# Four engines instead of one in written order: a scheduling change in the attention phase of a transformer block

## The chip, the core and the metric

The kernel runs on one core of one Trainium2 chip. The metric is device microseconds of one execution, smaller being better. Five engines work side by side, each through its own queue in order: TensorE (PE; its weight loads are listed as PEld), VectorE (DVE), ScalarE (ACT), GpSimd (POOL), and SyncE (SP), which here only issues DMA transfers. ScalarE's queue can issue transfers too. An instruction starts when the one ahead of it in its queue has started its turn and the semaphores that it waits for have been raised.

## The reference

Tokens S = 2048, width D = 576, one batch. Six vectors come from a condition vector `c`; a sliding-window attention block A and an MLP-mixer block B follow, each on a layer-normalised and modulated copy of x.

```python
mod = (silu(c) @ w_mod).reshape(1, 6, 1, D)
sa, ca, ga, sb, cb, gb = ...                      # its six rows
h = layernorm(x) * (1 + ca) + sa
x = x + ga * A(h)                                 # attention
h = layernorm(x) * (1 + cb) + sb
x = x + gb * B(h)                                 # mixer and MLP, F = 4608

# A: 32 heads of 18 columns, each token sees the 256 tokens up to itself
q, k, v = split(h @ wqkv)
p = softmax(where(0 <= i - j < 256, q @ k.T * 18 ** -0.5, -1e9))
A = (p @ v) @ wo
```

## The kernel before

All matrix products are kept close to float32 accuracy by writing each operand as a rounded high half and a low half (raw minus high half) and adding three products, so a contraction over 576 rows takes 14 matmuls (`products`). Making the two halves of an operand is called a split: ScalarE rounds (`split`, line 93), another engine subtracts (line 94).

Phase A (`phase_a`) is the attention. Tokens are treated in NB = 4 groups of 512. For each group the rows are normalised (`x_norm`: statistics on VectorE, lines 101 to 103, two small steps on GpSimd, 104 and 105, the scaling on ScalarE, 111), transposed on TensorE (`x_tr`, line 304), scaled and shifted by ScalarE (309), and split into `hT` by GpSimd (312) and VectorE (313). From `hT` nine q, k chunks of 128 columns (`qk_item`, line 321, 14 matmuls of 512 columns each) and eight v halves (`v_item`, 14 of 288 columns) are made. A q, k chunk leaves its PSUM bank through ScalarE and VectorE (lines 93 and 94, tile `qe`), goes to DRAM by transfers that ScalarE's queue issues (lines 348 to 354), and comes back rearranged by head (`pack`, lines 386 and 388, on SP's queue).

The attention itself is done in 32 units `u`, four heads and one group each. `scores` makes 16 score blocks of 128 x 384 (line 402); after each VectorE adds a mask and takes the row maximum (403). The maxima are negated, transposed and stored as two more rows of Q (`fin1`, `fin2`). `attend` makes the scores once more, transposed and with the maximum subtracted (436) and masked (445), ScalarE takes the exponential (449), TensorE multiplies with V (460), ScalarE copies the result out (465), and it is transposed and divided by its sum.

Beside this, `modvec` makes four of the modulation vectors on GpSimd (lines 492 and 494) from five loads each, and `s4` takes finished rows through the output projection: transposes and splits (71 to 79), 2 x 14 matmuls (627), addition of x (628), two normalisations with the modulation between them on GpSimd (638 and 639), stores. `load_w1` and `load_w2` bring and split the weights of the next phase. Phase B (`phase_bc`, `phase_b`) is the mixer, phase C (`phase_c`) the MLP.

The order of the work is written by hand: every step is put into a list `ev` with a time, whose unit is one attention unit u, and `play` calls them in the order of these times. `win` gives the stretches in which a group's projections are spread, `o_p`, `o_x`, `o_a` the offsets of loads, exponentials and products with V. For TensorE this order is binding:

```python
with self.tc.manual_schedule(engines={mybir.EngineType.PE}):
    play(ev)
```

The other queues are ordered by the framework's scheduler, which takes the written order as a priority and places what it estimates to be ready. In PSUM, `self.pb` gives the number of banks of each kind: `sc` 2 for score blocks, `st` 2 for the transposed scores, `av` 1, `mm` 2 for projections, `tr` 1 for transposes.

## Time and profile before

| what | value |
|---|---|
| median of three runs | 1886.11 us (1885.86 to 1888.06) |
| the profiled execution's own time | 1890.93 us |
| its span, first to last instruction | 1888.8 us |
| mean granted TensorE clock | 0.971 of full speed |
| busy: PE, DVE, ACT, POOL | 1774.5, 939.0, 635.6, 396.1 us |
| first copy of line 465 (end of the first unit) | 110.55 us |
| last copy of line 465 (end of the 32nd unit) | 783.22 us |

Busy times are sums over the whole span. A matmul of 128 x 512 is shown with about 0.4 us, but matmuls are pipelined, so a TensorE that is shown busy is not TensorE at its peak. In rows that list an instruction, the part in brackets is the idle time of its engine just ahead of it and what ended that; `x` with a number is how many instructions a row stands for.

### The profile page before, as it was taken

How to read it: one execution, taken by the hardware profiler on the slowest of the kernel's cores; microseconds unless marked ns; L12 is line 12 of the kernel's file. 1: busy time of each engine (PE TensorE's matmuls, PEld its weight loads, DVE VectorE, ACT ScalarE, POOL GpSimd, SP SyncE). 2: the span in 40 equal slices, each digit the busy share in tenths (PEclk: the TensorE clock that was granted, in tenths of full speed). 3: DMA queues.
4: the chain of work that ended last, by engine and by line, in shares of the span. 5: the costliest groups of instructions: out<-in, count | busy, mean ns of one | idle time of the engine just before them, and what ended most of it. 6: DMA issues, size and time to landing. Idle time of an engine off the chain costs nothing.

```text
span 1888.8 us, 29893 instructions
## 1 busy us (share of the span) xinstructions
PE 1774.5 (94%) x11504; PEld 1505.6 (80%) x11504; DVE 939.0 (50%) x2543; ACT 635.6 (34%) x1169; POOL 396.1 (21%) x430
## 2 busy tenths in 40 slices
PE   5889999999998888799989999999999999999999
PEld 3756766777776666588889999999999999999998
DVE  5445566555666666376754334343433434343333
ACT  3244454444554444443322222222222222222211
POOL 5030121111001222211232333332322222221100
PEclk7979999999999989899999999999999999999999
DMA  5533444424445443443421111110111000000002
GB/s 166 178 122 124 123 122 148 128 86 123 142 136 156 146 138 110 132 139 108 123 83 34 45 47 45 52 52 26 50 49 34 27 28 27 27 27 8 1 1 101
DMA packets 128117, 161.17 MB, mean 85 GB/s; under 512 B 35044, under 2 KB 69860, under 8 KB 127976
## 3 DMA queue, kind: packets, MB, share of 16 engines
q1 hardware_dynamic: 112616, 136.32, 24.7%
q10 hardware_dynamic: 15360, 22.95, 3.6%
q8 instruction: 91, 1.49, 0.3%
q14 instruction: 50, 0.41, 0.1%
HBM read 107.81 MB, written 50.73 MB: 84 GB/s over the span
## 4 chain that ended last, share of the span: by engine, by line
PE 80%; DVE 6%; DMA 5%; POOL 5%; issue 2%; ACT 2%; ACTq 0%; SPq 0%; POOLq 0%; DVEq 0%
PE p L911 24%; PE p L936 24%; PE qk L321 5%; PE sc L402 4%; PE X L436 4%; PE av L460 3%; PE pg L786 3%; PE po L627 2%; PE v L321 2%; PE X L445 2%; PE w L837 2%; DVE sc L403 1%; DMA wm<-in_w_mod_dram 1%; POOL s4rows L638 1%; POOL s4rows L639 1%
## 5 line engine op out<-in xcount | busy, mean ns | idle before, releaser
L911 PE MATMUL p<-LNT,W 128*128 128x512 f32 x2016 | 483.6, 391 | 0.0
L936 PEld LDWEIGHTS p<-W,Gc 128*128 128x128 f32 x3456 | 472.6, 188 | 11.1
L936 PE MATMUL p<-W,Gc 128*128 128x288 f32 x3456 | 480.4, 295 | 0.0
L911 PEld LDWEIGHTS p<-LNT,W 128*128 128x128 f32 x2016 | 372.0, 188 | 69.5
L403 DVE CUSTOM_DVE_ANT_0 sc<-sc,mask 128x384 f32<-128x384 f32 (+2 forms) x512 | 272.4, 541 | 188.7 <-PE sc L402 185.5
L915 ACT ACTIVATE gfc<-p 128x512 f32<-128x512 f32 x144 | 86.0, 597 | 663.4 <-PE p L911 663.4
L940 DVE TENSOR_TENSOR accA<-p,accA 128x288 f32<-128x288 f32 x340 | 151.5, 453 | 316.2 <-PE p L936 314.2
L449 ACT ACTIVATE P<-X 128x512 f32<-128x512 f32 (+2 forms) x384 | 216.2, 571 | 273.9 <-PE X L445 220.8
L402 PE MATMUL sc<-K,Q 108*128 108x384 f32 (+2 forms) x512 | 203.2, 399 | 33.7 <-DVE m L403 25.1
L940 DVE TENSOR_TENSOR accB<-p,accB 128x288 f32<-128x288 f32 x204 | 92.6, 455 | 198.1 <-PE p L936 196.1
L436 PE MATMUL X<-Q,K 110*128 110x128 f32 (+2 forms) x704 | 168.6, 315 | 11.0 <-ACT P L449 8.8
L321 PE MATMUL qk<-hT,Wc 128*128 128x512 f32 x504 | 163.4, 425 | 2.3 <-DVE hT L313 2.3
L436 PEld LDWEIGHTS X<-Q,K 110*128 110x128 f32 x704 | 128.2, 197 | 46.3 <-ACT P L449 17.9
L402 PEld LDWEIGHTS sc<-K,Q 108*128 108x128 f32 x512 | 101.0, 198 | 63.5 <-DVE m L403 39.8
L94 POOL TENSOR_TENSOR W<-r,W 128x576 fp32r<-128x576 f32 x34 | 49.1, 1443 | 466.8 <-ACT W L93 466.8
L445 PE MATMUL X<-maskb,identb 128*128 128x256 bf16 (+1 forms) x640 | 123.6, 259 | 0.0
L918 DVE TENSOR_TENSOR Gc<-gfc,Gc 128x512 fp32r<-128x512 f32 x144 | 118.2, 821 | 8.4 <-ACT Gc L917 4.7
L460 PE MATMUL av<-P,V 128*32 128x384 f32 (+2 forms) x1408 | 103.2, 406 | 0.0
L321 PEld LDWEIGHTS qk<-hT,Wc 128*128 128x128 f32 x504 | 88.8, 198 | 16.4 <-issue 4.8
L917 ACT CAST Gc<-gfc 128x512 fp32r<-128x512 f32 x144 | 89.3, 620 | 3.6
L321 PE MATMUL v<-Wv,hT 128*128 128x288 f32 x448 | 81.6, 305 | 0.5 <-ACT V L373 0.5
L627 PE MATMUL po<-Wo,oT 128*128 128x288 f32 x448 | 72.0, 312 | 2.1 <-DVE oT L79 1.5
(966 smaller groups left out, 1696.8 us busy)
## 6 DMA issues: line engine op xcount, KB each, us to landing
K<-k0d SPq DMA_DIRECT2D x96, 108.0 KB
r<-in_B_w_dram SPq DMA_DIRECT2D x36, 288.0 KB
Q<-q0d SPq DMA_DIRECT2D x128, 72.0 KB
K<-k1d SPq DMA_DIRECT2D x48, 108.0 KB
wm<-in_w_mod_dram SPq DMA_DIRECT2D x17, 288.0 KB
x<-in_A_x_dram SPq DMA_DIRECT2D x16, 288.0 KB
Q<-q1d SPq DMA_DIRECT2D x64, 72.0 KB
od<-o SPq DMA_DIRECT2D x32, 144.0 KB
```

The lines of the kernel that those rows point to most:

```text
L321: nc.tensor.matmul(pm, pl()[i][0], pl()[i][1], start=(i == 0), stop=(i == 13))
L402: nc.tensor.matmul(sc[:, lo:], q[0:2 * R3, h, i * P:(i + 1) * P], k[0:2 * R3, h // 2, i * P + lo:(i + 3) * P], start=True, stop=True)
L403: nc.vector.tensor_tensor_reduce(out=sc[:, lo:], in0=sc[:, lo:], in1=mask[:, lo:], scale=1.0, scalar=-3e38, op0=ALU.add, op1=ALU.max, accu ...
L436: nc.tensor.matmul(x[:, p0 * P:(p0 + w) * P], k[0:2 * R3 + 2, h // 2, (kb + 2) * P:(kb + 3) * P], q[0:2 * R3 + 2, h, q0 * P:(q0 + w) * P], ...
L445: nc.tensor.matmul(x[:, p0 * P:(p0 + w) * P], self.identb, m, start=False, stop=(n == len(ms) - 1))
L449: nc.scalar.activation(pt[:, c0:c1, h % 2, :], x[:, c0 * P:c1 * P].rearrange("p (a b) -> p a b", b=P), AF.Exp, scale=SCALE)
L460: nc.tensor.matmul(abox[0][32 * h:32 * h + 32, q0 * P:(q0 + w) * P], v[:, hh * VA:hh * VA + 32], Pt[b, h // 2][:, p0:p0 + w, h % 2, :], st ...
L627: nc.tensor.matmul(po, l, r, start=(n == 0), stop=(n == len(pl) - 1))
L911: nc.tensor.matmul(pg, w, a, start=(i == 0), stop=(i == len(pl) - 1))
L918: nc.vector.tensor_tensor(out=Gl, in0=gf, in1=Gh.bitcast(F32), op=ALU.subtract)
L936: nc.tensor.matmul(po, a, w, start=(i == 0), stop=(i == len(seq) - 1))
L940: nc.vector.tensor_tensor(out=acc[t][:, cs], in0=po, in1=acc[t][:, cs], op=ALU.add)
```

## The change

In phase A the order becomes binding for VectorE, ScalarE and GpSimd too, not for SP. Helpers that issued instructions on several engines at once are cut into steps of one engine, each with a time of its own, a little later than the step that it reads (`stat_steps`, `x_norm`, `x_tr`, `w_split`, `v_split`, `scores`, `attend`, `modvec`, `wo_one`, `load_chunk`). Engines change in some places: a q, k chunk is copied raw by ScalarE, rounded and subtracted by GpSimd, and stored by SP's queue; the subtractions of Wv, of the mixer's weights and of the first q chunk's weights go from VectorE to GpSimd. A score bank is added and a projection bank taken away. At the start `c` and the first rows are loaded ahead of `w_mod`, the warm-up matmuls come first, both first modulation vectors are summed on TensorE alone (`mod_sum`), and transposes precede the column extraction (`mod_col`). The first twelve tiles of the output projection have a version of their own, `s4a`: its products come in four parts, and its high half, like the low half of the first 512 columns, is made by GpSimd. The last four keep `s4`. In phases B and C `load_chunk` is called in three parts with the same instructions.

The core of the diff:

```diff
-        self.pb = {"sc": 2, "st": 2, "av": 1, "mm": 2, "tr": 1}
+        self.pb = {"sc": 3, "st": 2, "av": 1, "mm": 1, "tr": 1}
...
             def mod_sum(k):
                 def f():
                     kk = P if k < KC else TAIL
-                    w = wm["t"][:kk, k, :]
-                    for i, (c0, c1) in enumerate(half):
-                        if k == 0:
-                            wm[0, i] = ps([P, 512], "sc", f"pms{i}")
-                        nc.tensor.matmul(wm[0, i][:, 0:c1 - c0], wm["s"][:kk, k, :], w[:, c0:c1], start=(k == 0), stop=(k == KC))
-                    a = wm["a"][:kk]
-                    if k == 0:
-                        nc.vector.tensor_scalar(a, w[:, D:], silu[:kk, k:k + 1], None, op0=ALU.mult)
-                    else:
-                        nc.vector.scalar_tensor_tensor(out=a, in0=w[:, D:], scalar=silu[:kk, k:k + 1], in1=a, op0=ALU.mult, op1=ALU.add)
+                    for v in range(2):
+                        for i, (c0, c1) in enumerate(half):
+                            if k == 0:
+                                wm[v, i] = ps([P, 512], ("sc", "st")[v], f"pms{v}{i}")
+                            nc.tensor.matmul(wm[v, i][:, 0:c1 - c0], wm["s"][:kk, k, :], wm["t"][:kk, k, v * D + c0:v * D + c1], start=(k == 0), stop=(k == KC))
...
+            def w_split(c, t, lo):
+                def hi():
                     w, r = Wc[c], raws[c]
-                    self.split(w[:, 0:KC, :], w[:, KC:2 * KC, :], r[:, 0:KC, :], nc.scalar.copy, nc.vector.tensor_tensor)
-                    self.split(w[:, 2 * KC, :], w[:, 2 * KC + 1, :], r[:, KC, :], nc.scalar.copy, nc.vector.tensor_tensor)
-                return f
+                    nc.scalar.copy(w[:, 0:KC, :], r[:, 0:KC, :])
+                    nc.scalar.copy(w[:, 2 * KC, :], r[:, KC, :])
+
+                def low():
+                    w, r = Wc[c], raws[c]
+                    lo(out=w[:, KC:2 * KC, :], in0=r[:, 0:KC, :], in1=w[:, 0:KC, :].bitcast(F32), op=ALU.subtract)
+                    lo(out=w[:, 2 * KC + 1, :], in0=r[:, KC, :], in1=w[:, 2 * KC, :].bitcast(F32), op=ALU.subtract)
+                return [(t, hi), (t + self.g_w, low)]
...
+            def x_norm(t, t0):
+                bn, rs, nb, get = self.stat_steps(lambda: xrows[t], f"a{t}")
+                if t < 4:
+                    d = (0.0, 0.001, 0.015, 0.016)
+                    if t % 2:
+                        return [(t0, bn), (t0 + d[1], rs), (t0 + d[2], lambda: self.norm(xrows[t], xrows[t], get(), "v"))]
+                else:
+                    d = (0.0, 0.03, 0.12, 0.16)
+                return [(t0, bn), (t0 + d[1], rs), (t0 + d[2], nb), (t0 + d[3], lambda: self.norm(xrows[t], xrows[t], get()))]
...
+                if g == 0:
+                    a, b = (-8.92 + 0.001 * k, -8.84 + 0.01 * k) if k < KC else (-8.82, -8.79)
+                    return [(a, tr), (b, ev), (b + 0.001, hi), (b + 0.021, lo)]
+                return [(t0, tr), (t0 + 0.02, ev), (t0 + 0.06, hi), (t0 + 0.12, lo)]
...
-                def evac():
-                    pm = box["pm"]
-                    e = kp.tile([P, 2, 512], F32R, tag="qe", name=f"qe{g}_{c}", bufs=2)
-                    self.split(e[:, 0, :], e[:, 1, :], pm, nc.scalar.copy, nc.vector.tensor_tensor)
+                def raw():
+                    box["e"] = kp.tile([P, 2, 512], F32, tag="qe", name=f"qe{g}_{c}", bufs=2)
+                    nc.scalar.copy(box["e"][:, 1, :], box["pm"])
+
+                def hi():
+                    e = box["e"]
+                    nc.gpsimd.tensor_copy(e[:, 0, :].bitcast(F32R), e[:, 1, :])
+
+                def lo():
+                    e = box["e"]
+                    nc.gpsimd.tensor_tensor(out=e[:, 1, :].bitcast(F32R), in0=e[:, 1, :], in1=e[:, 0, :], op=ALU.subtract)
+
+                def store():
+                    e = box["e"]
                     f0 = c * P
                     nq = max(0, min(P, D - f0))
                     for u in range(2):
                         if nq:
-                            nc.scalar.dma_start(qd[g][u][f0:f0 + nq, :], e[:nq, u, :].bitcast(F32))
+                            nc.sync.dma_start(qd[g][u][f0:f0 + nq, :], e[:nq, u, :])
                         if nq < P:
                             k0 = f0 + nq - D
                             k1 = f0 + P - D
-                            nc.scalar.dma_start(kd[g][u][k0:k1, 256:], e[nq:, u, :].bitcast(F32))
+                            nc.sync.dma_start(kd[g][u][k0:k1, 256:], e[nq:, u, :])
                             if g < NB - 1:
-                                nc.scalar.dma_start(kd[g + 1][u][k0:k1, 0:256], e[nq:, u, 256:].bitcast(F32))
+                                nc.sync.dma_start(kd[g + 1][u][k0:k1, 0:256], e[nq:, u, 256:])
+                evac = [(0.01, raw), (0.04, hi), (0.08, lo), (0.12, store)]
...
+                e = []
+                for n, (i, h) in enumerate((i, h) for i in range(4) for h in range(4)):
+                    t = u - 1 + (n + 0.5) / 16
+                    e += [(t, one(i, h)), (t + 0.02, red(i, h))]
+                return e + [(u + 0.01, neg), (u + 0.1, mt), (u + 0.115, ms)]
...
+                e = []
+                for b in range(3):
+                    for h in range(4):
+                        t = u + self.o_x + (4 * b + h + 0.5) / 12
+                        e += [(t, xs(b, h)), (t + 0.015, ex(b, h))]
+                    e.append((u + self.o_x + (b + 1) / 3 + self.o_a, av(b)))
+                t = u + self.o_x + 1 + self.o_a
+                return e + [(t + 0.03, cp), (t + 0.15, ot), (t + 0.165, on)]
...
+                return [[(0.0, load(k)), (0.3, add(k))] for k in range(KC + 1)] + [bcast(0), bcast(1)]
...
+            ev = [(-9.5, warm(24)), (-9.45, consts), (-9.44, vones(0, 4)), (-9.4, c_load), (-9.2, wm_load), (-9.05, cond)]
+            ev += [(-7.4, lambda: clear(1)), (-7.35, lambda: clear(2)), (-1.2, vones(4, 10))]
+            for t in range(4):
+                ev += [(-9.3 + 0.01 * t, x_load(t))] + x_norm(t, -9.0 + 0.01 * t)
+            ev += [(-8.95 + 0.01 * k, mod_sum(k)) for k in range(3)] + [(-8.91 + 0.001 * k, mod_sum(3 + k)) for k in range(2)]
+            ev += [(-8.85 + 0.01 * j, mod_col(j)) for j in range(KC + 1)]
+            for k in range(KC + 1):
+                ev += x_tr(0, k, 0.0)
+            ev += [(wt[c], w_load(c)) for c in order]
+            ev += w_split(0, -8.9, nc.gpsimd.tensor_tensor) + w_split(4, -8.3, nc.vector.tensor_tensor) + w_split(5, -8.1, nc.vector.tensor_tensor)
+            for c in order[3:]:
+                ev += w_split(c, first[c][0] - 0.4, nc.vector.tensor_tensor)
+            ev += [(-8.75, v_load)]
+            for k in range(KC + 1):
+                ev += v_split(k, -7.9 + 0.05 * k)
...
-                    ev += [(tt - 1.2 + 0.1 * i, x_load(4 * g + i)), (tt - 0.6 + 0.1 * i, x_norm(4 * g + i))]
-                ev += [(w0 - 0.8 + 0.16 * k, x_tr(g, k)) for k in range(KC + 1)]
+                    ev += [(tt - 1.3 + 0.1 * i, x_load(4 * g + i))] + x_norm(4 * g + i, tt - 0.7 + 0.12 * i)
+                for k in range(KC + 1):
+                    ev += x_tr(g, k, w0 - 0.8 + 0.16 * k)
...
-            with self.tc.manual_schedule(engines={mybir.EngineType.PE}):
+                t0 = w1 + 0.85 + 0.72 * t
+                ev += [(t0 + d, f) for d, f in self.s4a(t, kp)]
+            ev += self.load_w1(w1 + 1.2, 0.56) + self.load_w2(w1 + 4.1, 0.6)
+            with self.tc.manual_schedule(engines={mybir.EngineType.PE, mybir.EngineType.DVE, mybir.EngineType.Activation, mybir.EngineType.Pool}):
                 play(ev)
 
     win = {1: (2.95, 9.0), 2: (9.8, 15.8), 3: (16.6, 22.4)}
-    o_p, o_x, o_a = 1.6, 0.38, 0.2
+    o_p, o_x, o_a, g_w = 1.6, 0.38, 0.18, 0.05
...
+        def wo(hf):
+            cs = slice(hf * 288, (hf + 1) * 288)
+
+            def part(a, b):
+                def f():
+                    T, W = box["T"], Wo["w"]
+                    if a == 0:
+                        box["po"] = ps([P, 288], "mm", f"po{t}_{hf}")
+                    pl = self.products(lambda k: T[:, k, :], lambda k: W[:, k, cs])
+                    for n in range(a, b):
+                        nc.tensor.matmul(box["po"], pl[n][0], pl[n][1], start=(n == 0), stop=(n == len(pl) - 1))
+                return f
+
+            def add():
+                x = box["x"]
+                nc.vector.tensor_tensor(out=x[:, cs], in0=box["po"], in1=x[:, cs], op=ALU.add)
+                if hf == 1:
+                    nc.sync.dma_start(self.xp[t], x)
+            return [part(a, b) for a, b in ((0, 4), (4, 8), (8, 11), (11, 14))], add
...
+        e = [(-0.7, load_o), (0.1, load_x)]
+        for t0, st in ((0.0, tr(False)), (0.16, tr(True))):
+            e += list(zip((t0, t0 + 0.015, t0 + 0.05, t0 + 0.09), st))
+        for hf, t0 in enumerate((0.28, 0.5)):
+            st, add = wo(hf)
+            e += spread(st, t0, t0 + 0.2) + [(t0 + 0.205, add)]
+        e += [(0.9, b1), (0.93, r1), (1.02, n1), (1.04, lambda: self.norm(x(), x(), g1())), (1.1, mod)]
+        e += [(1.4, b2), (1.43, r2), (1.52, n2), (1.54, ln2)]
+        return e
...
+        def one(fc, t):
+            src = self.w1[:, 144 * fc:144 * fc + P] if fc < KC else self.w1
+            load, hi, lo = self.load_chunk(f"W1{fc}", src, nc.scalar.copy, nc.gpsimd.tensor_tensor, fc == KC)
+
+            def begin():
+                with nc.allow_non_contiguous_dma("sixteen columns of a shift group"):
+                    self.W1[fc] = load()
+            return [(t, begin), (t + 0.8, hi), (t + 0.85, lo)]
```

More of the change, by code (lines that the diff above doesn't have):

```diff
@@ L555, in put @@
+            for k in range(KC + 1):
+                ev += v_split(k, -7.9 + 0.05 * k)
+            def put(it, t0, t1):
                 steps, evac = it
-                return spread(steps, t0, t1) + [(t1, evac)]
+                return spread(steps, t0, t1) + [(t1 + d, f) for d, f in evac]
             for c in order:
@@ L582, in phase_a @@
[L582 to L589 removed]
+                ev.append((u - self.o_p if u else -7.3, pack(u)))
@@ L590, in phase_a @@
+                ev += scores(u) + attend(u)
             for n, v in enumerate((2, 3, 4, 5)):
-                ev += spread(modvec(v), 3.0 + 3.2 * n, 6.0 + 3.2 * n)
+                for k, f in enumerate(modvec(v)):
+                    t = 3.0 + 3.2 * n + 0.4 * k
+                    ev += [(t + d, e) for d, e in f]
             w1 = self.win[NB - 1][1]
-            ev += [(w1 - 0.3, wo_begin), (w1 + 0.03, s4_begin)] + [(w1 - 0.2 + 0.12 * k, wo_one(k)) for k in range(KC + 1)]
+            ev += [(w1 - 0.35, wo_begin), (w1 + 0.03, s4_begin)]
@@ L673, in load_w1, with hi, lo @@
+        def hi():
+            h(box["w"][:, 0:KC, :], box["r"][:, 0:KC, :])
+            h(box["w"][:, 2 * KC, :], box["r"][:, KC, :])
+        def lo():
+            w, r = box["w"], box["r"]
+            l(out=w[:, KC:2 * KC, :], in0=r[:, 0:KC, :], in1=w[:, 0:KC, :].bitcast(F32), op=ALU.subtract)
+            l(out=w[:, 2 * KC + 1, :], in0=r[:, KC, :], in1=w[:, 2 * KC, :].bitcast(F32), op=ALU.subtract)
+        return load, hi, lo
+    def load_w1(self, t0, dt):
         nc = self.nc
         self.W1 = {}
-        def one(fc):
-            def f():
-                if fc < KC:
-                    self.W1[fc] = self.load_chunk(f"W1{fc}", self.w1[:, 144 * fc:144 * fc + P], nc.scalar.copy, nc.vector.tensor_tensor)
-                else:
-                    with nc.allow_non_contiguous_dma("sixteen columns of a shift group"):
-                        self.W1[fc] = self.load_chunk(f"W1{fc}", self.w1, nc.scalar.copy, nc.vector.tensor_tensor, True)
-            return f
```

320 lines of the change are left out of this document (189 added, 131 removed).

## The prediction

> **What bounds the kernel now.** I read the page's slices first, then the busy time by stretch, then the starts of one instruction that marks each unit of attention, then who waited for whom, and last the order of time where TensorE stood still. Columns of the slices: one digit per 47 us, tenths of busy time, and the granted TensorE clock below.
>
> ```profile
> PE   5889999999998888799989999999999999999999
> PEclk7979999999999989899999999999999999999999
> ```
>
> From the 21st slice on TensorE is full at full clock: that is the second half of the network, which the change leaves as it is. What can move lies in the first 800 us. The next view gives busy time by stretch (stretch, its length, then PE, PEld, DVE, ACT and POOL with counts, the granted clock, the DMA share and GB/s). Its cuts after 110 us are starts of line 465, the copy that ends a unit of four heads.
>
> ```profile
> 44.00:110.55 66.55, 60.27 (x334) 48.06 (x335) 35.32 (x126) 21.04 (x44) 6.81 (x13) 0.90 0.55 171
> 110.55:163.94 53.39, 41.80 (x251) 29.04 (x251) 27.11 (x100) 24.70 (x45) 13.39 (x21) 0.81 0.37 113
> 255.94:305.56 49.62, 42.48 (x308) 30.47 (x308) 29.84 (x93) 22.83 (x39) 13.09 (x17) 0.97 0.47 139
> 407.13:455.69 48.56, 41.72 (x299) 30.26 (x300) 25.75 (x80) 21.10 (x36) 8.69 (x9) 0.93 0.44 119
> 455.69:556.49 100.80, 98.59 (x779) 76.61 (x780) 65.16 (x205) 55.69 (x104) 0.00 (x0) 1.00 0.45 124
> 579.70:748.55 168.85, 143.94 (x1128) 111.74 (x1129) 105.37 (x364) 77.73 (x136) 40.17 (x56) 0.93 0.46 138
> ```
>
> ```profile
> 455.69 0.59 ACT L465 COPY avs<-av 128x512 f32<-128x512 f32 x1 [2.65 <-PE av L460]
> ...
> 556.49 0.59 ACT L465 COPY avs<-av 128x512 f32<-128x512 f32 x1 [0.33 <-PE av L460]
> 579.70 0.59 ACT L465 COPY avs<-av 128x512 f32<-128x512 f32 x1 [3.45 <-PE av L460]
> ...
> 748.55 0.59 ACT L465 COPY avs<-av 128x512 f32<-128x512 f32 x1 [0.45 <-PE av L460]
> ```
>
> The copy of 556.49 is the fifth after that of 455.69, the one of 748.55 the seventh after 579.70. So an undisturbed unit takes 100.80 / 5 = 20.2 us, with TensorE busy 98% at full clock: there is little to win in such a unit. The stretches 110 to 164, 256 to 306 and 407 to 456 hold two units each and are 53.4 - 40.4 = 13.0, 9.2 and 8.2 us longer than that, 30.4 in sum; they are where the rows of the next group of tokens are normalised and transposed. The seven units to 748.55, in which the output projection runs beside attention, are 168.85 - 7 x 20.2 = 27.5 us too long. TensorE is the bound of a good unit; the waste lies in these places, and there it is the order of the other engines' queues. Three of them in order of time (start, length, what, idle before and its releaser):
>
> ```profile
> 131.45 0.74 POOL L492 TENSOR_SCALAR wm<-wm,silu 64x576 f32<-64x576 f32 x1 [2.86 <-DMA wm<-in_w_mod_dram]
> 133.61 0.60 POOL L312 CAST hT<-h 128x512 fp32r<-128x512 f32 x1
> 134.25 0.69 DVE L313 TENSOR_TENSOR hT<-h,hT 128x512 fp32r<-128x512 f32 x1 [5.28 <-POOL hT L312]
> 135.39 0.58 PE L402 MATMUL sc<-K,Q 108*128 108x256 f32 x1 [4.33 <-DVE m L403]
> ```
>
> GpSimd stands at a modulation row whose transfer has not landed, the rounded half of hT comes late behind it, VectorE stands at the low half, the score reductions stand behind that, and TensorE has no free score bank for 4.33 us. Over the whole span such waits sum to (us, times, longest)
>
> ```profile
> PE sc L402 <- DVE m L403: 25.1, 21, 4.3
> ```
>
> ```profile
> 300.77 0.52 ACTq L348 DMA_DIRECT2D q0d<-qe  x1
> ...
> 303.94 0.61 ACTq L354 DMA_DIRECT2D k1d<-qe  x1
> 304.59 1.09 ACT L449 ACTIVATE P<-X 128x512 f32<-128x512 f32 x2 [3.85 <-DMA K<-k0d]
> 305.24 0.30 PEld L436 LDWEIGHTS X<-Q,K 110*128 110x128 f32 x2 [2.00 <-ACT P L449]
> ```
>
> Here ScalarE's queue issues the stores of one q, k chunk for 3.8 us, its exponentials wait, and TensorE with them.
>
> ```profile
> 640.68 0.46 DVE L101 BATCH_NORM_STATS2 c3st<-s4rows 128x6 f32<-128x288 f32 x1 [1.58 <-POOL s4rows L639]
> 643.99 0.39 PE L77 MATMUL oTT4pb<-ident,s4rows 128*64 128x128 f32 x1 [3.81 <-DVE oT L73]
> 646.79 3.12 PE L627 MATMUL po<-Wo,oT 128*128 128x288 f32 x14
> ```
>
> And here a normalisation that waits for GpSimd stands in VectorE's queue ahead of work that TensorE needs; then fourteen matmuls run as one block.
>
> **The change part by part.** The order of TensorE's steps stays nearly the same; new is that VectorE, ScalarE and GpSimd follow the written order as well, with each helper cut into steps that come a few hundredths of a unit after what they read.
>
> The start. Today the last rows are normalised late, since GpSimd's small steps stand between its memsets, and the first chunk's copy is at 44.62, the first score at 64.21:
>
> ```profile
> 32.58 1.37 POOL L167 MEMSET K<- 32x1536 f32 x1
> 32.63 1.64 DVE L113 TENSOR_SCALAR x<-x,a3mv,a3rs 128x576 f32<-128x576 f32 x1
> 34.33 3.89 PE L304 MATMUL hT<-ident,x 128*128 128x128 f32 x17 [2.50 <-DVE x L113]
> 44.62 0.59 ACT L93 CAST qe<-qk 128x512 fp32r<-128x512 f32 x1 [0.20 <-DVE Wv L94]
> 64.21 0.22 PE L402 MATMUL sc<-K,Q 108*128 108x128 f32 x1
> ```
>
> The new order loads c and the rows before the modulation weights, normalises and transposes while these come, and has only five column extractions, scalings and splits behind them. From the transposes at 34.33 to the copy are 10.3 us; I let nine of them go (between 4 and 11): -9. Against that, the first eight projections have no score work between them and now only one bank. Prices of a copy that empties a bank, and of the moved halves (group; busy us, mean ns; idle before):
>
> ```profile
> L93 ACT CAST qe<-qk 128x512 fp32r<-128x512 f32 x36 | 21.1, 585 | 21.7 <-PE qk L321 14.7 <-DMA k0d<-qe 3.7 <-DMA K<-k0d 1.2
> L373 ACT COPY V<-v 128x288 f32<-128x288 f32 x32 | 12.8, 400 | 15.2 <-PE v L321 14.7
> L628 DVE TENSOR_TENSOR s4rows<-po,s4rows 128x288 f32<-128x288 f32 x24 | 11.0, 457 | 26.8 <-PE po L627 26.8
> L94 DVE TENSOR_TENSOR qe<-qk,qe 128x512 fp32r<-128x512 f32 x36 | 24.8, 688 | 11.1 <-ACT qe L93 11.0
> L312 POOL CAST hT<-h 128x512 fp32r<-128x512 f32 x16 | 10.1, 636 | 69.3 <-ACT h L309 69.2
> L94 POOL TENSOR_TENSOR W<-W_0r,W 128x512 fp32r<-128x512 f32 x5 | 6.4, 1284 | 1.1 <-ACT W L93 1.1
> ```
>
> Eight times about 0.5 us and a hand-over (0.20 us stands ahead of the copy at 44.62) is +6, bounded by 0 (if the first scores are waiting for their transfers anyway) and 8. In the rest of the opening stretch TensorE idles 66.55 - 60.27 = 6.3 us, mostly with two score banks full; three banks and no late splits ahead of the reductions should take two thirds: -4 (0 to -6).
>
> The group borders. Modulation rows are now multiplied 0.3 of a unit (6 us) after their load is issued, statistics are spread by 0.12 of a unit, and a row's normalisation follows its statistics by 0.16. One such load took about this long:
>
> ```profile
> 122.97 3.28 DMA wm<-in_w_mod_dram
> ```
>
> So GpSimd should no longer stand there. Of the 30.4 us I take two thirds, -20 (between -8 and all of it), since the chain scale, round, subtract over one shared buffer stays.
>
> The q, k halves. VectorE loses 36 x 0.688 = 24.8 us, GpSimd gains 36 x (0.636 + 1.284) = 69.1 us, and a chunk reaches its store 1.2 us later. GpSimd is busy 40.17 of 168.85 us where it has most to do in the long stretches above, so there is room, and what hides the delay is the chunk's lead of over a unit on its first reader; with no lead it would cost up to 1.2 x 36 = 43 us. I take 0. The stores leave ScalarE's queue for SP's, where they can stand behind a load that waits for its Q buffer; two staging buffers and some 14 us between chunks (two thirds of a unit in the windows) cover that. The stall at 300.77 goes, but most chunks issue fewer stores and good units are 98% full: -1 (0 to -5).
>
> One projection bank, later on. In the windows an item's matmuls end a tenth of a unit (2 us) before the next begins, against 0.6 us for the copy, so it is mostly hidden: +3. If none of it is hidden, the sum of the rows is 36 x 0.585 + 32 x 0.40 + 24 x 0.457 = 44.9 us.
>
> The output projection beside attention. Its fourteen matmuls come in four parts, its splits lie on GpSimd but for the tail, and normalisation steps are put where their inputs are ready. Of the 27.5 us I take three quarters: -21 (between -10 and all of it).
>
> A rule weighed. More GpSimd time may slow VectorE: the normalisation at 32.63 took 1.64 us beside a GpSimd memset, its twin this long without one:
>
> ```profile
> 29.60 0.57 DVE L113 TENSOR_SCALAR x<-x,a1mv,a1rs 128x576 f32<-128x576 f32 x1
> L403 DVE CUSTOM_DVE_ANT_0 sc<-sc,mask x512: 273/566/600, 64.5 to 758.1; 128x384 f32<-128x384 f32 x150, 128x128 f32<-128x128 f32 x11, 128x256 f32<-128x256 f32 x10
> ```
>
> The 512 score reductions, which read one operand from PSUM, never took over 600 ns (least, median, most) though GpSimd worked beside many of them. I therefore charge nothing for them. The Trainium skill, in "SBUF — State Buffer", section "Who interferes with whom", says that a VectorE instruction with two SBUF inputs, or in a two-port mode, and a GpSimd instruction exclude each other, while one with at most one SBUF input is left alone; by that rule the trace agrees, and the remaining low halves on VectorE would be the ones to suffer.
>
> The sum is -9 + 6 - 4 - 20 + 0 - 1 + 3 - 21 = -46 us. The profiled execution took 1890.93 us, with a span of 1888.8; the sum makes that 1844.9. The median of the three runs, 1886.11, lies 4.8 lower, and 1886.1 - 46 = 1840.1.
>
> **The rivals.** First, the projection bank takes the place of the score bank. Against it speaks the 2 us between items, for it that ScalarE's copies now wait their turn behind exponentials of 0.6 us. With all 44.9 us shown instead of the 9 charged, the gain is 46 - 36 = 10 us: 1876. That the written order turns out much like the order that the queues have today ends in the same place, since then only the start and the stores move.
>
> Second, slower: GpSimd becomes the head of the line. Every q, k half now stands in the same queue as twenty modulation rows that wait for transfers and the row splits that TensorE waits for. If rows land later than 6 us after their issue, the chain seen at 131 to 135 us comes back, with scores behind it. One such place cost half of the 13.0 us found from 110 to 164, so 6.5 us. Seven places (46 / 6.5 = 7.1) eat the whole gain; nine give 9 x 6.5 - 46 = +12: 1898. For it speaks that SP's queue keeps its own order and now carries the stores; against it the 3.28 us of a load, and that only twenty such rows exist.
>
> Third, low halves held up by GpSimd. VectorE keeps 20 of hT, 18 of the q, k weights and 5 of Wo. If each waits for a GpSimd subtraction of 1.284 us in three cases of ten, and TensorE waits with it, that is 43 x 1.284 x 0.3 = 17 us: 1886.1 - 46 + 17 = 1857. This is the case in which that rule of the Trainium skill reaches TensorE.
>
> Fourth, more is won: all of the 30.4 and 27.5 us, 11 at the start and 5 at the stores. That is 30.4 + 27.5 + 11 + 5 + 6 less nothing for the bank, 80 us: 1806.
>
> **How the numbers follow.** The forecast, 1840, has a chance of 0.53; with its recovered shares moved by a third either way its own range is 1822 to 1858. The first rival has 0.16, of which 0.03 within 0.2% (3.8 us, about what can be told from no change), the second 0.13, the third 0.05, the fourth 0.13. Faster: 0.53 + 0.13 + 0.05 + 0.13 = 0.84; same 0.03; slower 0.13. The range runs from 1797, a little below the fourth case, to 1882, above the first; it leaves out the second and the tail below.
>
> **What would show it.** Right: the span after the 21st slice unchanged; the first copy of a q, k chunk near 36 us; the stretches at the group borders within 3 or 4 us of two good units; the seven units beside the output projection near 21 us each; no stores on ScalarE's queue; waits of the score matmul for the reduction well under the 25 us of the TensorE rows today. Wrong: a good unit longer than 20.2 us, waits of projection matmuls for the copies of lines 93 or 373 of tens of us, or VectorE and ScalarE standing behind GpSimd's halves while the granted clock falls under 0.9 beside them.

## The result and the profile after

The changed kernel takes 1821.5 us (median of 4 runs, 1820.7 to 1822.48); the kernel before, run beside it on the same chip, 1885.98 us (4 runs). The ratio is 0.9659, 95% interval 0.9642 to 0.9676: 64.5 us less. Its profiled execution took 1821.39 us, its span is 1819.6 us, and the mean granted TensorE clock is 0.991. The slices of TensorE and its granted clock, changed kernel, 45 us to a digit:

```profile
PE   8899999999998897999899999999999999999999
PEclk9999999999999998999999999999999999999999
```

The 5 at the left is an 8 now, and of the four low clock digits one 8 is left. The busy time by stretch, changed kernel, columns as before. The cuts are starts of the copy that ends a unit (line 537 now, first row), chosen to hold the same units as the stretches of before:

```profile
L537 ACT COPY avs<-av x32: 565/585/592, 94.2 to 710.4; 128x512 f32<-128x512 f32 x32
```

```profile
44.00:94.19 50.19, 44.45 (x275) 35.53 (x274) 26.03 (x102) 16.08 (x37) 17.15 (x20) 0.97 0.56 176
94.19:129.45 35.26, 33.30 (x247) 23.77 (x248) 23.35 (x88) 21.31 (x40) 11.76 (x18) 1.00 0.51 156
129.45:226.16 96.71, 91.79 (x671) 68.29 (x671) 54.68 (x194) 42.23 (x87) 32.92 (x36) 1.00 0.47 131
226.16:264.22 38.06, 37.18 (x295) 28.07 (x294) 25.71 (x85) 22.47 (x39) 14.82 (x20) 1.00 0.52 158
264.22:369.75 105.53, 101.84 (x793) 78.94 (x794) 60.84 (x200) 49.12 (x87) 28.79 (x34) 1.00 0.42 122
369.75:408.74 38.99, 37.69 (x297) 28.39 (x298) 24.63 (x77) 21.77 (x37) 8.73 (x11) 1.00 0.46 133
408.74:510.01 101.27, 99.16 (x790) 77.68 (x790) 55.34 (x181) 48.75 (x89) 18.52 (x18) 1.00 0.37 102
510.01:525.33 15.32, 14.13 (x117) 10.33 (x117) 13.12 (x43) 9.67 (x19) 5.33 (x5) 0.89 0.66 191
525.33:678.34 153.01, 136.68 (x1139) 107.64 (x1139) 101.85 (x353) 81.60 (x149) 73.84 (x97) 0.98 0.61 171
710.43:1819.60 1109.17, 1083.14 (x6496) 984.17 (x6496) 490.66 (x1049) 284.87 (x528) 257.77 (x237) 0.99 0.17 52
```

The last stretch of the kernel before, and two of its stretches between the borders, for comparison:

```profile
163.94:255.94 92.00, 90.61 (x665) 67.80 (x664) 53.42 (x190) 41.04 (x86) 9.40 (x9) 1.00 0.43 127
305.56:407.13 101.57, 99.69 (x783) 77.59 (x782) 56.77 (x186) 46.35 (x85) 11.60 (x11) 1.00 0.40 117
783.22:1888.80 1105.58, 1084.05 (x6496) 984.84 (x6496) 490.48 (x1048) 284.99 (x528) 256.79 (x236) 0.99 0.17 52
```

The same cuts in all profiles give this table (us of one profiled execution each; "u0" is the end of the first unit, "borders to u16" the sixteen units with the three borders, "u22" the single unit before the output projection is fully under way, "seven" the seven units beside it). Where an edit does not reach, stages differ between builds by up to 4.4 us (the tails of the builds of the changed kernel), so smaller differences are not read.

| kernel | median | u0 | borders to u16 | five good units | u22 | seven | last two | tail |
|---|---|---|---|---|---|---|---|---|
| before | 1885.98 | 110.6 | 345.1 | 100.8 | 23.2 | 168.8 | 34.7 | 1105.6 |
| changed | 1821.5 | 94.2 | 314.6 | 101.3 | 15.3 | 153.0 | 32.1 | 1109.2 |
| e1, only PE bound | 1868.32 | 111.5 | 323.5 | 100.1 | 17.6 | 173.7 | 34.4 | 1106.8 |
| e10, PE and VectorE bound | 1832.57 | 107.5 | 319.6 | 99.0 | 17.8 | 147.5 | 31.1 | 1107.8 |
| e7, VectorE free | 1859.22 | 96.1 | 321.8 | 101.3 | 16.5 | 175.6 | 37.1 | 1111.2 |
| e8, ScalarE free | 1823.02 | 97.9 | 315.1 | 100.8 | 15.3 | 152.9 | 31.1 | 1106.9 |
| e9, GpSimd free | 1825.71 | 101.7 | 316.3 | 99.9 | 16.2 | 146.2 | 31.9 | 1109.0 |
| e2, two score banks | 1824.37 | 98.0 | 316.5 | 101.4 | 16.5 | 152.9 | 32.0 | 1111.2 |
| e3, halves on VectorE | 1828.05 | 93.9 | 321.0 | 100.8 | 18.2 | 153.3 | 31.8 | 1110.6 |
| e4, stores on ScalarE | 1839.91 | 101.1 | 330.4 | 101.6 | 15.3 | 148.1 | 31.8 | 1109.0 |
| e5, before, all bound | 1956.78 | 110.7 | 363.0 | 107.6 | 18.2 | 208.4 | 40.0 | 1103.7 |
| i1, start banks | 1818.73 | 95.3 | 316.0 | 101.3 | 15.3 | 149.4 | 32.1 | 1109.9 |
| i2, x rows early | 1819.38 | 94.4 | 317.2 | 101.3 | 16.2 | 147.3 | 31.8 | 1108.1 |
| i3, both and two more | 1816.01 | 89.1 | 314.5 | 101.3 | 16.2 | 148.1 | 31.8 | 1109.6 |

From before to changed: the start -16.4, the sixteen units -30.5, u22 -7.9, the seven -15.9, the last two -2.6, the good units +0.5, the tail +3.6. That is the 69.2 us by which the span is shorter. What TensorE waited for, changed kernel (us, times, longest; line 455 is the score matmul, 462 its reduction):

```profile
PE po L750 <- DVE s4rows L755: 7.6, 8, 3.0
PE xnT1pa L71 <- DVE xnT L73: 5.4, 1, 5.4
PE v L363 <- ACT qe L384: 2.9, 6, 0.7
PE qk L363 <- ACT qe L384: 1.4, 2, 0.7
PE qk L363 <- DVE hT L352: 1.0, 2, 0.6
PE sc L455 <- DVE m L462: 0.2, 1, 0.2
```

The score matmuls' wait for the reduction, 25.1 us before, has fallen to 0.2 us (once).

Not all of the gain is idle time. Up to the last copy of a unit, before and then changed (columns as above):

```profile
0.00:783.22 783.22, 690.50 (x5008) 520.79 (x5008) 448.53 (x1496) 350.59 (x641) 139.29 (x194) 0.94 0.44 132
0.00:710.43 710.43, 661.98 (x5024) 503.97 (x5024) 419.12 (x1418) 347.03 (x642) 258.08 (x323) 0.99 0.50 145
```

Of the 72.8 us won there, 44.3 are idle time of TensorE (92.7 against 48.4 us). The other 28.5 us are TensorE's own work, which is shorter with a few matmuls more, at a granted clock of 0.99 in place of 0.94.

### The profile page after: what moved, and what is told of

It is laid out like the page before. It is cut to its first block, busy times and chain, and to the rows that moved or that the text cites. A ratio compares the mean times of both kernels' runs of the same rounds, so it can differ in the third digit from the quotient of the medians.

```text
span 1819.6 us, 30069 instructions
## 1 busy us (share of the span) xinstructions
PE 1745.1 (96%) x11520; PEld 1488.1 (82%) x11520; DVE 909.8 (50%) x2467; ACT 631.9 (35%) x1169; POOL 515.9 (28%) x559
## 4 chain that ended last, share of the span: by engine, by line
PE 82%; DVE 5%; POOL 4%; DMA 4%; ACT 2%; issue 2%; SPq 1%; ACTq 0%; POOLq 0%; DVEq 0%
PE p L1136 25%; PE p L1111 25%; PE qk L363 5%; PE av L532 4%; PE X L502 4%; PE sc L455 4%; PE v L363 2%; PE X L511 2%; PE pg L983 2%; PE po L750 2%; PE w L1034 2%; DMA wm<-in_w_mod_dram 1%; DVE sc L462 1%; POOL wm L581 1%; PE oT L543 1%
## 5 line engine op out<-in xcount | busy, mean ns | idle before, releaser
L1111 PEld LDWEIGHTS p<-LNT,W 128*128 128x128 f32 x2016 | 371.5, 188 | 69.2
L455 PE MATMUL sc<-K,Q 108*128 108x384 f32 (+2 forms) x512 | 191.7, 382 | 5.8 <-DMA k0d<-qe 3.3
L94 POOL TENSOR_TENSOR W<-r,W 128x576 fp32r<-128x576 f32 x34 | 48.6, 1429 | 466.0 <-ACT W L93 465.9
L502 PE MATMUL X<-Q,K 110*128 110x128 f32 (+2 forms) x704 | 163.0, 306 | 3.7 <-ACT P L521 3.4
L363 PE MATMUL qk<-hT,Wc 128*128 128x512 f32 x504 | 159.4, 414 | 3.6 <-ACT qe L384 1.4
L502 PEld LDWEIGHTS X<-Q,K 110*128 110x128 f32 x704 | 123.9, 191 | 28.7 <-issue 9.4
L388 POOL CAST qe<-qe 128x512 fp32r<-128x512 f32 x36 | 22.2, 616 | 256.3 <-ACT qe L384 241.2
```

What stands on the lines that cost most here:

```text
L363: nc.tensor.matmul(pm, pl()[i][0], pl()[i][1], start=(i == 0), stop=(i == 13))
L455: nc.tensor.matmul(sc[:, lo:], q[0:2 * R3, h, i * P:(i + 1) * P], k[0:2 * R3, h // 2, i * P + lo:(i + 3) * P], start=True, stop=True)
L502: nc.tensor.matmul(x[:, p0 * P:(p0 + w) * P], k[0:2 * R3 + 2, h // 2, (kb + 2) * P:(kb + 3) * P], q[0:2 * R3 + 2, h, q0 * P:(q0 + w) * P], ...
L1111: nc.tensor.matmul(pg, w, a, start=(i == 0), stop=(i == len(pl) - 1))
```

## The experiments

Three theories were put up. Q: the gain is the binding order of the other queues. B: it is the third score bank. M: it is the moved work (q, k halves on GpSimd, stores off ScalarE). Every edit is made to the changed kernel, but for e5, which edits the kernel before. In the cuts of the code `mybir.EngineType.` is left out, and some lines are shortened (`...`) or noted (`#`).

**Which part carries the gain (e1 to e4).** e1 leaves everything as changed but binds TensorE's queue alone:

```diff
-with self.tc.manual_schedule(engines={PE, DVE, Activation, Pool}):
+with self.tc.manual_schedule(engines={PE}):
```

> The changed kernel, with only TensorE's order binding again; the steps stay split and on their new engines, three score banks stay. Theory Q (the written order of the three other queues carries the gain): most of the 64 us come back, 1860 to 1885 us, and the score matmuls wait for reductions again by 10 us or more. Theory B (the third score bank carries it): 1815 to 1830 us, with that wait still under 2 us. Theory M (moved work: halves on GpSimd, stores on SP, carries it): 1815 to 1835 us.

Measured: 1868.32 us, ratio to before 0.9901 (0.9884 to 0.9917). It gives back 46.8 of the 64.5 us: the start is again where it was (111.5), the seven units are longer than before (173.7). What TensorE waits for most in e1:

```profile
PE po L750 <- DVE s4rows L755: 14.8, 9, 3.0
PE sc L455 <- DVE m L462: 9.6, 9, 2.7
```

Though the third score bank is there, the scores wait for the reduction again, 9.6 us, just under the 10 expected. Q holds for the start and the seven units. What e1 keeps, 17.7 us, lies mostly in the sixteen units, 323.5 against 345.1 us, with steps cut and work moved but not bound. So of the 30.5 us won in these units and borders, 21.6 do not need the binding order.

```diff
-self.pb = {"sc": 3, "st": 2, "av": 1, "mm": 1, "tr": 1}
+self.pb = {"sc": 2, "st": 2, "av": 1, "mm": 2, "tr": 1}
```

(e2; the transpose that used a score bank at the start uses the second projection bank.)

> The changed kernel with two score banks and two projection banks, as before; one transposed tile of the start moves from a score bank to a projection bank. Theory Q: within 12 us of the changed kernel, 1815 to 1833 us; the start is 3 to 6 us shorter as the first eight projections have two banks, and waits of score matmuls for reductions grow to 5 to 15 us. Theory B: 1850 us or more, with those waits back at 25 us. Theory M: 1821 us.

Measured: 1824.37 us, 0.9675 (0.9655 to 0.9695), 2.9 us above the changed kernel. TensorE's wait in e2:

```profile
PE sc L455 <- DVE m L462: 10.1, 15, 2.5
```

Of ten microseconds of returned waits little reaches the end; the intervals of e2 and of the changed kernel overlap, so the exchange of a bank carries nothing that these runs can tell from zero. The edit gives back the second projection bank as well, and with it TensorE's waits for lines 384 and 755 are gone; what the third score bank is worth by itself was not run. The start, expected 3 to 6 us shorter, is 3.8 us longer.

```diff
-evac = [(0.01, raw), (0.04, hi), (0.08, lo), (0.12, store)]
+evac = [(0.01, hi), (0.04, lo), (0.06, store)]   # hi: ScalarE from PSUM, lo: VectorE from PSUM
```

(e3.)

> The changed kernel, with the two halves of a q, k chunk made as before, rounded by ScalarE and subtracted by VectorE out of PSUM; the stores stay on SP's queue. Theory Q: 1815 to 1830 us, since VectorE has room; each chunk reaches its store about 1.2 us earlier, and the start may be 3 us shorter. Theory M: 1835 us or more, as 25 us come back to VectorE.

Measured: 1828.05 us, 0.9689 (0.9671 to 0.9708): 6.5 us come back, in the borders, though the interval still touches the changed kernel's (up to 0.9676). The start, which was to be up to 3 us shorter, stays. TensorE's waits in e3:

```profile
PE v L363 <- DVE qe L388: 11.4, 15, 1.4
PE qk L363 <- DVE qe L388: 3.8, 4, 1.6
```

The one projection bank is now held until VectorE has subtracted; with the raw copy it is free when ScalarE is done. By the trace that is what the move to GpSimd buys, rather than VectorE's time: 15.2 us of waits for the chunk's halves, against 4.3 for line 384 in the changed kernel.

```diff
-nc.sync.dma_start(qd[g][u][f0:f0 + nq, :], e[:nq, u, :])
+nc.scalar.dma_start(qd[g][u][f0:f0 + nq, :], e[:nq, u, :])
```

(e4; the k stores likewise.)

> The changed kernel with the stores of the q, k chunks issued by ScalarE's queue again, where they now also wait for GpSimd's halves. Theory Q: slower by 5 to 20 us, 1826 to 1842 us, since a wait for GpSimd now stands in the queue of the exponentials. Theory M (stores as the main term): 1845 us or more. If ScalarE has room for all of it: 1819 to 1825 us.

Measured: 1839.91 us, 0.9753 (0.9738 to 0.9767): 18.4 us come back, in the start and the borders. ScalarE in order of time in e4, and its largest new waits:

```profile
150.92 0.34 ACTq L404 DMA_DIRECT2D k0d<-qe  x1
...
152.80 0.66 ACT L521 ACTIVATE P<-X 128x256 f32<-128x256 f32 x2 [2.71 <-DMA k0d<-qe]
...
163.84 0.49 ACT L521 ACTIVATE P<-X 128x384 f32<-128x384 f32 x1 [1.56 <-POOL qe L392]
```

```profile
ACT P L521 <- POOL qe L392: 11.7, 8, 1.8
ACT P L521 <- DMA k0d<-qe: 7.1, 3, 2.7
```

The exponentials stand behind the issues, and more often behind a store that waits for GpSimd's low half. The second is new in e4: before, no half of a chunk was GpSimd's. So 18.4 us is the price of stores on ScalarE beside halves on GpSimd, not of the stores alone. Stores on ScalarE beside halves made as before were not run.

**Whether a binding order pays by itself (e5).** The kernel before, its steps uncut, with the other three queues bound. Q1: any written order does; Q2: only one whose steps are cut and spread.

```diff
-with self.tc.manual_schedule(engines={PE}):
+with self.tc.manual_schedule(engines={PE, DVE, Activation, Pool}):
```

> The kernel before, unchanged but that the written order binds VectorE, ScalarE and GpSimd too; steps stay whole, so an exponential stands right behind its matmuls and a normalisation's VectorE steps right behind one another, with GpSimd's steps between them. Theory Q1 (binding alone carries it): 1835 to 1855 us. Theory Q2 (binding pays only with the steps cut and spread): 1870 us or more, even slower than before, with VectorE standing at lines 106, 313 and 73 by more than 40 us and TensorE behind it.

Measured: 1956.78 us, 1.036 (1.0335 to 1.0384), 68 us slower than the kernel before beside it (1888.64). Waits of TensorE, of VectorE and of GpSimd in e5 (its line numbers are those of before):

```profile
PE sc L402 <- DVE m L403: 46.5, 48, 3.8
```

```profile
DVE s4rows L628 <- PE po L627: 43.3, 22, 3.8
DVE hT L313 <- POOL hT L312: 30.5, 18, 4.4
```

```profile
POOL hT L312 <- ACT h L309: 66.2, 17, 10.3
```

A helper that issues on three engines puts VectorE's part into VectorE's queue at once, however late the other engine's part is that it waits for: 18 times, up to 4.4 us, for hT, and longest for the output projection (43.3 us, 26.8 before). The score reductions stand behind that. It is not the second rival's chain: GpSimd's rounding of hT waits for ScalarE (line 309), never for a modulation row. Q2 fits: binding wins 46.8 us with steps cut and loses 68 with steps whole. But the two kernels differ in engines and banks as well, so that the cutting makes the difference is likely, not isolated.

**Whose queue it is (e7 to e10).** One engine is left to the scheduler in e7 (VectorE), e8 (ScalarE) and e9 (GpSimd); in e10 only TensorE and VectorE are bound. The theory V: VectorE's queue carries most of it.

```diff
-with self.tc.manual_schedule(engines={PE, DVE, Activation, Pool}):
+with self.tc.manual_schedule(engines={PE, Activation, Pool}):    # e7
+with self.tc.manual_schedule(engines={PE, DVE, Pool}):           # e8
+with self.tc.manual_schedule(engines={PE, DVE, Activation}):     # e9
+with self.tc.manual_schedule(engines={PE, DVE}):                 # e10
```

> The changed kernel with VectorE's queue left to the scheduler, the other three bound. Theory V (VectorE's queue carries most of the 47 us that the order is worth): 1845 to 1865 us, and the score matmuls wait for reductions by 8 us or more. If the three queues share it evenly: 1832 to 1842 us. If another queue carries it: 1819 to 1828 us.

> The changed kernel with ScalarE's queue left to the scheduler, the other three bound. Theory V: 1821 to 1832 us. Even shares: 1832 to 1842 us. If ScalarE's queue carries it (the exponentials stand behind normalisations and splits): 1845 us or more.

> The changed kernel with GpSimd's queue left to the scheduler, the other three bound. Theory V: 1819 to 1830 us. Even shares: 1832 to 1842 us. If GpSimd's queue carries it (halves behind modulation rows): 1845 us or more.

> The changed kernel with the written order binding TensorE and VectorE alone; ScalarE and GpSimd are left to the scheduler. If VectorE's queue by itself carries what the order is worth: 1821 to 1832 us. If it needs the other two bound as well (the three single releases sum to 44 of 47 us, so little is shared): 1835 to 1850 us.

Measured: e7 1859.22 us (0.9839, 0.9809 to 0.987), 37.7 us above the changed kernel (34 by the ratios); e8 1823.02 (0.9657, 0.963 to 0.9683), 1.5 above, and e9 1825.71 (0.967, 0.9646 to 0.9694), 4.2 above, both with intervals that overlap the changed kernel's; e10 1832.57 (0.9718, 0.9697 to 0.9739), 35.8 of e1's 46.8 us; it lies between the two ranges expected. V holds, but not by the wait that was expected with it, 8 us or more of the scores for the reduction. TensorE's waits in e7:

```profile
PE po L750 <- DVE s4rows L755: 19.2, 9, 4.5
PE sc L455 <- DVE m L462: 2.7, 3, 1.2
```

The order of time in e7, beside the output projection:

```profile
574.57 0.46 DVE L103 BATCH_NORM_STATS2 c1st<-s4rows 128x6 f32<-128x288 f32 x1 [2.22 <-POOL s4rows L766]
...
576.70 0.45 DVE L755 TENSOR_TENSOR s4rows<-po,s4rows 128x288 f32<-128x288 f32 x1
577.21 1.33 PE L750 MATMUL po<-Wo,oT 128*128 128x288 f32 x4 [4.45 <-DVE s4rows L755]
581.72 0.60 ACT L521 ACTIVATE P<-X 128x512 f32<-128x512 f32 x1 [8.05 <-PE X L511]
```

The scheduler puts a normalisation that waits 2.22 us for GpSimd ahead of the addition that empties the one projection bank; TensorE stands for 4.45 us, ScalarE for 8.05 us. The seven units take 175.6 us in e7, 147.5 in e10: there it is VectorE's order that counts. The start is another matter: it needs the other two, since e10 ends its first unit at 107.5, 13.3 us late, while freeing ScalarE or GpSimd alone costs 3.7 and 7.5 us there, the first no more than builds differ.

**What the prediction left open (i1 to i3).** i1 gives two of the first q, k chunks and two v halves another bank, so that the first projections alternate; i2 issues the load of x for the output projection 0.45 of a unit earlier; i3 does both, makes the low half of Wv on VectorE, and one weight step of phase B later.

```diff
-box["pm"] = ps([P, 512], "mm", f"qk{g}_{c}")
+box["pm"] = ps([P, 512], "av" if g == 0 and c in (4, 1) else "mm", f"qk{g}_{c}")    # i1, i3; v halves 0 and 3 likewise
...
-e = [(-0.7, load_o), (0.1, load_x)]
+e = [(-0.7, load_o), (-0.35, load_x)]                                               # i2, i3
...
-nc.gpsimd.tensor_tensor(out=w[:, l, :], ...)
+nc.vector.tensor_tensor(out=w[:, l, :], ...)                                        # i3
...
-ev = [(-1.5, begin), (-0.9, w2t), ...]
+ev = [(-1.5, begin), (-0.1, w2t), ...]                                              # i3
```

> The changed kernel; four of the first eight projections (two q, k chunks and two v halves) use the bank that the product with V does not need yet. The prediction's +6 for one bank at the start, if right: 3 to 6 us less, 1815 to 1819 us, and the first score near 49 us instead of 53. If the first scores wait for GpSimd's halves and the transfers anyway: 1820 to 1823 us.

> The changed kernel; the x rows of the output projection are loaded 0.45 of a unit earlier. In the changed kernel's trace VectorE stood 3.2 us at one such row and TensorE 2.96 us behind it at half clock afterwards. If that is the cause of the long unit that ends at 574.9: 3 to 7 us less, 1814 to 1818 us. If SP's queue then delays other loads instead: 1820 us or more.

> Both edits together, and the low halves of Wv on VectorE again (it idles there, and GpSimd's subtraction of Wv delays the halves of the second chunk by 5.6 us), and the sixteen-column weights of the mixer split after its first transposes instead of ahead of them. If each is worth what the trace shows as a stall: 8 to 15 us less, 1806 to 1814 us. If they hide one another: 1814 to 1820 us.

Measured: i1 1818.73 us (0.9635, 0.9619 to 0.9651), i2 1819.38 (0.9636, 0.9621 to 0.965), i3 1816.01 (0.962, 0.9604 to 0.9636). The first two have intervals that overlap the changed kernel's, and i2 lies between its two expected ranges; i3 lies in the range for edits that hide one another. The first score matmul in the changed kernel, in i1 and in i3, order of time:

```profile
53.44 0.23 PE L455 MATMUL sc<-K,Q 108*128 108x128 f32 x1
```

```profile
53.68 0.30 PE L455 MATMUL sc<-K,Q 108*128 108x128 f32 x1 [2.04 <-DMA Q<-q0d]
```

```profile
47.69 0.30 PE L455 MATMUL sc<-K,Q 108*128 108x128 f32 x1 [1.98 <-DMA Q<-q0d]
```

More banks do not bring the first score forward: it waits for a transfer of Q. The 2.8 us by which i1's median is lower show in the seven units, which its edit does not touch, so I do not credit them to the banks. In i3 the score comes 5.8 us earlier, and its first unit ends 5.1 us earlier; i1 and i2 do not move that point, so Wv's low halves are needed for it; whether they do it without i1's banks was not run. i3 is the fastest version, 5.5 us below the changed kernel.

## Why the prediction was right, and where its sizes were off

The direction and the range held: 1821.5 lies in 1797 to 1882, 18.5 us below the forecast. The mechanism held in the main: the binding order carries 46.8 of the 64.5 us (e1). The sum came as near as it did in part by luck: the start and the units to u22 won 30 us more than their terms, the output projection and the tail 9 less. Step by step:

**The start, -9 + 6 - 4, measured -16.4.** The order of time of the changed kernel at the start:

```profile
29.25 0.58 ACT L384 COPY qe<-qk 128x512 f32<-128x512 f32 x1 [1.33 <-PE qk L363]
...
31.96 5.57 POOL L303 TENSOR_TENSOR Wv<-wvr,Wv 128x576 fp32r<-128x576 f32 x4
37.47 0.62 POOL L388 CAST qe<-qe 128x512 fp32r<-128x512 f32 x1
```

The first copy comes at 29.25, not near 36: 15.4 us earlier than before, beyond the bound of 11, since the transposes, which the term left at 34.33, moved forward too, to 15.99. The +6 for one bank was the wrong cost: i1 shows nothing near it, and its lower bound, 0, fits, for the reason given there, the transfers. But 4.6 us of the 15.4 were lost before the first score, and a place that the term did not have accounts for it as far as i3 shows: four low halves of Wv stand in GpSimd's queue for 5.57 us, ahead of the halves of the next chunk, which ScalarE had copied from 33.40 on. By the first score 10.8 us are won (53.44 against 64.21), the other 5.6 from there to the end of the first unit (-4 forecast).

**The group borders, -20, and what was left out, measured -38.4 with u22.** The stretches of two units fell from 53.4, 49.6 and 48.6 us to 35.3, 38.1 and 39.0, by 39.3 us: more than the 30.4 that I held to be all, because two such units take 35 to 39 us when little disturbs them, and not 40.4: they hold 247 to 297 matmuls, two good units 316. In turn the stretches between them grew from 92.0 and 101.6 to 96.7 and 105.5 us, 8.7 in sum, and GpSimd's busy time in the first of them from 9.40 to 32.92 us. The net, -30.5 with the stores and the bank in it, stands against -20 - 1 + 3 = -18. The size that failed is the share: two thirds was a guess at what the chain over a shared buffer would keep, and nearly all went. The mechanism named for it, the order of the queues, holds in part: e1 keeps 21.6 of the 30.5 us with TensorE's queue alone bound, so the cut steps, the moved work or the third bank carry more here than the binding; which of them is open. The unit from 556.49 to 579.70, 23.2 us, was in no term; it fell by 7.9 us.

**The q, k halves, 0.** The groups in the changed kernel (busy us, mean ns; idle before):

```profile
L388 POOL CAST qe<-qe 128x512 fp32r<-128x512 f32 x36 | 22.2, 616 | 256.3 <-ACT qe L384 241.2 <-DMA Q<-q0d 10.0 <-DMA Q<-q1d 5.0
L392 POOL TENSOR_TENSOR qe<-qe 128x512 fp32r<-128x512 f32 x36 | 46.6, 1296 | 2.4
```

They cost GpSimd 68.8 us (69.1 forecast) and nothing on the path. But the term missed a gain: by e3 the raw copy, which frees the bank sooner, is worth some 6 us, at the edge of what the runs can tell.

**The stores, -1.** Undersized, by how much can't be said: e4's 18.4 us holds the new wait for GpSimd.

**One projection bank later, +3.** The waits for line 384 above sum to 4.3 us, but the output projection's matmuls wait another 7.6 us for line 755, which empties the same bank; before, none waited for it in these units. Of these, 2.96 us go back to a row of x (below). So the waits come to more than 3, some of it in the seven units; the first rival (44.9 us) is out.

**The output projection, -21, measured -15.9.** The seven units take 21.9 us each, near the 21 forecast. Part of the rest is a row of x that lands late, in the changed kernel at

```profile
562.04 0.46 DVE L755 TENSOR_TENSOR s4rows<-po,s4rows 128x288 f32<-128x288 f32 x1 [3.17 <-DMA s4rows<-in_A_x_dram]
562.55 1.33 PE L750 MATMUL po<-Wo,oT 128*128 128x288 f32 x4 [2.96 <-DVE s4rows L755]
```

The step counted the addition as ready; its other operand comes by a transfer. From 562.1 to 568.9 us, so from the end of this stop on, the granted clock is 0.50; if the stop brings that with it, which no run isolates, it costs more than its own 2.96 us. Such waits for x stand in the traces of the changed kernel, e2, e8 and i1 (1.8 to 7.7 us in sum), whose seven units take 149.4 to 153.0 us; in e4 there is one of 0.7 us, in e9, e10, i2 and i3 none, and they take 146.2 to 148.1. But e3 has none either and takes 153.3, with a stop of TensorE of 3.01 us for a transfer of Q. With the load earlier (i2) they take 147.3 us, 21.5 below before; but e4, e9 and e10 have no earlier load, so where the row lands depends on more than that, e3 shows that it is not the only cause, and i2's median is only 2.1 us lower, within the intervals.

**The span after attention, 0, measured +3.6.** In the changed kernel the first wait of phase B's transposes is 5.4 us (the row of xnT1pa above); in e1 this stretch takes 1106.8, in e5 1103.7 us; 3.6 us is no more than builds differ. That the new order ends its rows later is argued only, and i3's edit did not shorten it (1109.6). This stays open.

**Good units:** 101.27 / 5 = 20.3 us, unchanged as forecast. **Third rival:** the mechanism is there, but not its price: TensorE waited for VectorE's part of hT for 1.0 us in all. Its count was off as well: the change leaves VectorE 16 low halves of q, k weights, not 18, and the twelve of line 737, two of which were held up (last section), were left out. **What kept the score reductions on time** is neither the order of VectorE's queue nor the bank alone: the scores wait for them 9.6 us with three banks and TensorE alone bound (e1), 10.1 us with all queues bound and two banks (e2), and 2.7 us with three banks and only VectorE free (e7). What VectorE's order keeps on time is the addition of line 755 (19.2 us of TensorE's waits in e7, 7.6 with it).

## What to carry to other kernels

When several queues wait for each other, look at who stands at the head of each: a bound order pays where each helper is cut into steps of one engine, each placed a little after what it reads, and can cost more where it is not (46.8 us won by e1's comparison, 68 lost in e5). Of the engines off the bound, bind first the one whose queue holds both work that TensorE waits for and work that waits for others, here VectorE. And price a block of small steps that stands ahead of an urgent one as an item of its own: four halves of Wv stood 5.57 us ahead of a chunk here, and i3, which moves them, starts 5 us sooner.

## What the runs showed of the hardware

A short VectorE instruction with two operands in SBUF took up to five times as long here beside a GpSimd subtraction. The changed kernel in order of time, and all instructions of that line (least, median, most ns):

```profile
555.42 1.26 POOL L857 TENSOR_TENSOR W<-W10r,W 128x512 fp32r<-128x512 f32 x1
555.46 1.37 DVE L737 TENSOR_TENSOR oT<-oh,oT 64x128 fp32r<-64x128 f32 x1 [0.71 <-POOL oT L732]
...
606.92 1.42 POOL L895 TENSOR_TENSOR W<-rw,W 128x576 fp32r<-128x576 f32 x1
606.98 1.50 DVE L737 TENSOR_TENSOR oT<-oh,oT 64x128 fp32r<-64x128 f32 x1 [0.72 <-POOL oT L732]
```

```profile
L737 DVE TENSOR_TENSOR oT<-oh,oT x12: 284/286/1502, 524.2 to 694.1; 64x128 fp32r<-64x128 f32 x12
L462 DVE CUSTOM_DVE_ANT_0 sc<-sc,mask x512: 291/565/601, 53.7 to 685.7; 128x384 f32<-128x384 f32 x150, 128x128 f32<-128x128 f32 x11, 128x256 f32<-128x256 f32 x10
```

Ten of the twelve had no GpSimd instruction beside them and took 0.28 to 0.29 us; these two took 1.37 us beside GpSimd's 1.26 and 1.50 beside 1.42. The score reductions, with one operand in PSUM, never took over 0.601 us, though 222 of the 512 had GpSimd work beside them (76 before). So the rule of the Trainium skill that the prediction weighed ("SBUF — State Buffer", "Who interferes with whom") holds here in both its parts; with two SBUF inputs the page puts it for a GpSimd instruction that reads SBUF, as these subtractions do. An instruction so held ends some 0.15 us after GpSimd's; these two began with it, so they waited for nearly the whole of it.
